# Attention and mixture of experts on one core: other token order inside a batch, gate weights stored in 16-byte pieces

## The chip, the cores and the metric

The kernel runs on one core of one Trainium2 chip. The metric is device time in microseconds (us); lower is better. A core has five engines with queues of their own: TensorE (PE; its weight loads are shown apart as PEld), VectorE (DVE), ScalarE (ACT), GpSimd (POOL) and SyncE (SP), which here issues most of the transfers. All transfers, whoever issues them, run on the same 16 DMA engines.

## The reference

Capped attention over 8 batches, 12 heads, 448 tokens and 64 columns a head; then one expert for each of the 3584 tokens, at most 80 tokens an expert.

```python
scores = cap * np.tanh((q @ k.T / 8) / cap)          # per batch and head
attn = softmax(scores)                               # over the keys
x = (attn @ v)  -> [3584 tokens, 768]
logits = x @ w_gate                                  # [3584, 8]
expert_idx = argmax(logits); gate_w = softmax(logits)[expert_idx]
for e in range(8):                                   # keep the 80 tokens with the largest gate_w
    h = relu(x[tok] @ w1[e]); out[tok] = gate_w[tok] * (h @ w2[e])
```

All other rows of the output are zero.

## The kernel before

**Attention stage (0 to some 391 us).** 48 steps, one for each batch b (8) and pair of heads (6). TensorE makes scores (`sc`, L1019) and products with the values (`av`, L1043); ScalarE does tanh and exp; GpSimd and VectorE add the row sums. SP loads `kt`, `qt` (three steps ahead) and `vr` (one ahead).

**Gate of a batch (8 times).** When the six 128x448 blocks `x` of a batch are there, TensorE multiplies them with the gate's weights (`lgp`), ScalarE copies the logits to `lgs` (96 partitions x 448 tokens), and TensorE turns them in four transposes (L1126): the tokens then stand on 112 partitions (`C`) and 4 columns (`NC`) of `lt`. In a transpose, the 96x112 piece of `lgs` is the stationary operand (the LDWEIGHTS), and the identity is the moving one. VectorE works out expert, sorting key (`kc`) and gate weight on those 112x4 numbers, and `gate_weights` stores the gate weights `g` in the list `gd` in memory (L322), one float for each of the 3584 tokens. For batches 0 to 6 SP issues this store, for batch 7 GpSimd does. Later each expert's rows of `x` (`xge`, `xgv`, from the copy `xs`) and of `gd` (`gt`, `gtv`) are gathered by token number. A constant table (`pa`, `pb`, from the number t4 = 4 (token + 1)) says which token stands at which partition and column.

**Expert stage (391 to 516 us).** Six experts' products in a fixed order, `hp` (x by w1) and `yt` (by w2), both issued at L758. Each takes its weights `w` from memory in 84 loads by SP (L746) of 512 or 384 KB, in a ring of buffers, each load waiting for the fifth before it. The last batch's gate, ranking and stores to `xs` (8 of them, from GpSimd's queue) go on beside this. The order of instructions on every engine is written out by the program, not by a scheduler that weighs costs.

The lines the steps touch are the view of `gd`, the transposes, and the store:

```python
gdv = gd.rearrange("(c p) a -> p (c a)", p=C)            # token = 112 c + p
nc.tensor.transpose(lt[:, c]..., lg[:, c * C:(c + 1) * C], cst("ident", 96)[:, :96])
queue.dma_start(gdst, g)                                 # gdst = gdv[:, 4 columns of batch b]
```

Of the kernel before, what the change touches and what calls it, by code (L numbers as in the profile page):

```python
# [17 lines left out]
B, H, S, D = 8, 12, 448, 64  # L18
NP = H // 2
NQ = H // 4  # L20
C = 112
# [3 lines left out]
NC = S // C  # L25
NB = S // 32
T = B * S
NCOL = T // C
DM = H * D
E = 8  # L30
# [52 lines left out]
def const_table():  # L83
    import numpy as np
    t = np.zeros((128, NCT), np.float32)

    def put(key, val):
        a, b = CT[key]
        t[:, a:b] = val
    p = np.arange(128)  # L90
    e = np.arange(E)
    put("pow", np.exp2(31.0 * e - 98.0)[None])
    put("rev", (E - e)[None])
    put("pre", (e < NPRE)[None])
    put("pen", (E * (e >= NPRE))[None])
    put("io", e[None])
    put("io32", np.arange(32)[None])
    put("io96", np.arange(SL)[None])
    put("lo3", np.array([[0, 32, 64]]))
    put("hi3", np.array([[32, 64, 96]]))  # L100
    put("slot", p[:, None])
    t4 = 4 * (p[:, None] + C * np.arange(NCOL)[None] + 1)
    put("pa", t4 // 256 * 256)
    put("pb", t4 % 256)
    put("blk", SL * np.arange(NBMAX)[None])
    put("gt", (e[None, :] > e[:, None]).reshape(1, -1))
    put("tri", np.where(np.arange(C)[None, :] >= p[:, None], -1.0, 0.0))
    put("rest", (T - C * (np.arange(NCOL) + 1))[None])
    put("ident", np.eye(128))
    return t  # L110
# [3 lines left out]
def attn_moe(ctx, tc, q2, k, v, cap, wg, w1, w2, capacity, ct, out):  # L114
    nc = tc.nc
# [4 lines left out]
    ohd = dram.tile([C, NCOL, E], F32, name="ohd")  # L120
    xs = dram.tile([T, 4, NP, 32], F32, name="xs")
    gd = dram.tile([T, 1], F32, name="gd")
    gdv = gd.rearrange("(c p) a -> p (c a)", p=C)

    fl_i = consts.tile([1, 2], I32, name="fl_i")
    big = consts.tile([1, 1], F32, name="big")
# [14 lines left out]
    def cst(key, n=128):  # L141
        a, b = CT[key]
        return ctt[:n, a:b]
# [6 lines left out]
    kc = consts.tile([C, NCOL], F32, name="kc")  # L150
    oh = consts.tile([C, NCOL, E], F32, name="oh")
    cms = consts.tile([C, OCOL], F32, name="cms")
    ohv = consts.tile([C, WCOL, E], F32, name="ohv")
    cmn = consts.tile([C, WCOL], F32, name="cmn")
# [3 lines left out]
    us = consts.tile([C, OCOL], F32, name="us")  # L158
# [677 lines left out]
    def attention_rowmax(sm, pl, b):  # L836
# [3 lines left out]
        for u in range(NQ):  # L840
            xp = [pl.tile([128, 512], F32, name=f"gxp{u}{f}", tag=f"gxp{f}") for f in range(2)]
            for h4 in range(4):
# [11 lines left out]
                for i in range(NC):  # L854
                    ps = pl.tile([C, 512], F32, name=f"gps{j}{h}{i}", tag="gps")
                    nc.tensor.matmul(ps[:, :S], qt[:, h, i * C:(i + 1) * C], kt[:, h, :], start=True, stop=True)
                    e = sm.tile([C, S], F32, name=f"ge{j}{h}{i}", tag="ge")
# [30 lines left out]
        lg = sm.tile([32, S], F32, name="glgs", tag="glgs")  # L888
        nc.vector.tensor_copy(lg, lgp[0:32, :S])
        lt = pl.tile([C, NC, 1, 32], F32, name="glt", tag="glg", bufs=2)  # L890
        for c in range(NC):
            nc.tensor.transpose(lt[:, c, 0], lg[:, c * C:(c + 1) * C], cst("ident", 32)[:, :32])
        kcb = sm.tile([C, NC], F32, name="gkc", tag="gkc")
        ohb = sm.tile([C, NC, E], F32, name="goh", tag="goh")
        for f in gate_math(sm, lt[:, :, :, 0:E], "g", kcb, ohb, gdv[:, bass.ds(b * NC, NC)]):
            f()
        nc.sync.dma_start(kcd[:, bass.ds(b * NC, NC)], kcb)
        nc.sync.dma_start(ohd[:, bass.ds(b * NC, NC)], ohb)
# [1 line left out]
    def general():  # L900
# [4 lines left out]
        with tc.If(bg > 0):  # L905
            with tc.tile_pool(name="gs", bufs=1) as sm:
                with tc.tile_pool(name="gp", bufs=1, space=PSUM) as pl:
                    with tc.For_i(0, B, 1) as b:
                        attention_rowmax(sm, pl, b)
                    nc.sync.dma_start(kc, kcd)  # L910
                    nc.sync.dma_start(oh, ohd)
# [48 lines left out]
    sm = at.enter_context(tc.tile_pool(name="sm", bufs=2))  # L960
# [8 lines left out]
    st = {"laid": set()}  # L969
# [4 lines left out]
    with ExitStack() as a2:  # L974
# [123 lines left out]
        def stored(q, b, i, js=slice(0, NB)):  # L1098
            q.dma_start(xs.rearrange("(b j a) i p c -> b i a j p c", b=B, j=NB)[b, i, :, js], st["xt", b][32 * i:32 * i + 32, js])
# [7 lines left out]
        def logits(b, js):  # L1107
            if js[0] == 0:
                st["lp", b] = ps1.tile([128, 512], F32, name=f"lgp{b}", tag="misc", bufs=2)
            for j in js:  # L1110
                g = j % 3
                nc.tensor.matmul(st["lp", b][32 * g:32 * g + 32, :S], wgt[:, j, :], st["x", b, j], start=(j < 3), stop=(j >= 3))

        def gate(b):
            def product():
                logits(b, range(NP))
                lp = st["lp", b]
                lg = sm.tile([96, S], F32, name=f"lgs{b}", tag="lgs", bufs=1)
                nc.scalar.copy(lg, lp[0:96, :S])
                st["lgs", b] = lg  # L1120

            def turn():
                lg = st["lgs", b]
                lt = ps1.tile([C, NC, 3, 32], F32, name=f"lt{b}", tag="misc", bufs=2)
                for c in range(NC):
                    nc.tensor.transpose(lt[:, c].rearrange("p g e -> p (g e)"), lg[:, c * C:(c + 1) * C], cst("ident", 96)[:, :96])  # L1126
                st["lt", b] = lt

            def math():
                cs = slice(b * NC, (b + 1) * NC)  # L1130
                lt = st["lt", b][:, :, :, 0:E]
                if b < OB:
                    st["math"] = gate_math(sm, lt, b, kc[:, cs], oh[:, cs], gdv[:, cs], us[:, cs], cms[:, cs])
                else:
                    ws = slice(b * NC - OCOL, (b + 1) * NC - OCOL)
                    st["math"] = gate_math(sm, lt, b, kc[:, cs], oh[:, cs], gdv[:, cs], None, cmn[:, ws], ohv[:, ws], nc.sync if b < B - 1 else nc.gpsimd)
            def end(pd):
                r = st["rank"] = consts.tile([C, RCOL], F32, name="rank")
                nc.vector.tensor_tensor(osd, osd, dfc2, op=ALU.add)
                nc.vector.tensor_reduce(r, acc2, axis=AX.X, op=ALU.add)  # L1140
                nc.vector.tensor_tensor(r, r, osd, op=ALU.subtract)
                n = pd.shape[-1]
                nc.vector.tensor_tensor(r[:, :n], r[:, :n], pd, op=ALU.subtract)
                st["chain"]()
            def later():
                st["math"][2]()
                if b < OB:
                    steps = list(ranks(krow, gp, ps1, "misc", b, acc, dfc, 0, 0, []))
                else:
                    steps = list(ranks(krow, gp, ps1, "misc", b, acc2, dfc2, CAND, OCOL, [e * SL for e in range(E)]))  # L1150
                if b == OB - 1:
                    kept = list(prune(krow, gp, ps1, "misc"))
                    n = next(i for i, x in enumerate(kept) if x[0] == 1750)
                    steps = [steps[0], kept[0], *steps[1:4], kept[1], *steps[4:7], kept[2], *steps[7:9], *kept[3:n], *steps[9:], *kept[n:]]
                if b > OB:
                    bg.insert(0, steps.pop(0))
                bg.extend(steps)
                now[2] = now[0]
                ready_at[2] = clock[1]

            def finish():
                st["math"][2]()
                steps = list(ranks(krow, gp, ps1, "misc", b, acc2, dfc2, CAND, OCOL, [e * SL for e in range(E)], end=end))
                f0, f1, f2, f6, f3, f4, f5, f8 = final_order(sm, lambda: ps1.tile([128, 512], F32, name="pcn", tag="misc", bufs=2))
                parts = [(50, lambda i=i, h=h: stored(nc.gpsimd, b, i, slice(NB // 2 * h, NB // 2 * h + NB // 2)), 1) for i in range(4) for h in range(2)]
                head = [(400, f0, 0), steps[0], (200, f1, 1), steps[1], (200, f2, 1), steps[2], (200, f6, 1), (200, f3, 0), steps[3],
                        steps[4], (300, f4, 1), *steps[5:8], (300, f5, 1), *steps[8:10], (300, f8, 1), *steps[10:]]
                n = 4
                for x in parts:
                    head.insert(n, x)  # L1170
                    n += 2
                bg.extend(head)
            st["wait"]()
            urgent.append((300, product, 0 if b < OB else 1))
            urgent.append((300, turn, 1 if b < OB else 2))
            if b < OB - 1:
                urgent.append((2500, lambda: (math(), st["math"][0](), st["math"][1](), later()), 1))
                return
            urgent.append((1900, lambda: (math(), st["math"][0]()), 1 if b < OB else "ordered"))
            urgent.append((1900, lambda: st["math"][1](), 0))  # L1180
            urgent.append((1000, finish if b == B - 1 else later, 0))
# [242 lines left out]
```

## Time and profile before

| | us |
|---|---|
| three runs: median (lowest to highest) | 524.43 (523.38 to 525.9) |
| the profiled execution | 523.92 |
| its span, first to last instruction | 522.1 |
| TensorE busy | 477.3 (91%) |
| VectorE / ScalarE / GpSimd busy | 344.2 / 328.6 / 257.4 |
| mean granted TensorE clock | 0.992 |

The profile is of one execution; 1.8 us of its time lie around the span. A busy TensorE is not one at its peak, since matmuls are pipelined. The profile's 40 slices of the span show TensorE busy in nine tenths or more of nearly each slice up to about 420 us, and 7 to 9 tenths behind that.

### The profile page before, as it was taken

To read this page: it belongs to the slowest core of one execution; us is meant where nothing else is said; L and a number is where in the kernel's file an instruction comes from. 1 tells how busy PE (TensorE), PEld (TensorE's weight loads), DVE (VectorE), ACT (ScalarE), POOL (GpSimd) and SP (SyncE) were. 2 spreads that over 40 slices of the span, in tenths; PEclk is the share of its full clock that TensorE was granted. 3 is DMA by queue.
4 is the path that set the end of the run, shared out by engine and by line. 5 is a ranking of instruction groups with operands and counts; after the bars stand their busy time and mean duration, and the time that the engine had idled before them with its cause. 6 is when DMAs were issued, how large, how long until landed. Compare 5 with 4: busy or idle time off the path is not lost. (4 is left out here: it accounts for less than half of the span.)

```text
span 522.1 us, 13512 instructions
## 1 busy us (share of the span) xinstructions
PE 477.3 (91%) x5476; PEld 218.7 (42%) x5476; DVE 344.2 (66%) x783; ACT 328.6 (63%) x326; POOL 257.4 (49%) x175
## 2 busy tenths in 40 slices
PE   6899999999899999999999998989999978887894
PEld 2223322332332323333323332233335778787894
DVE  1177789878988998899889866984669624512000
ACT  4998879788787978788777875857890101011111
POOL 0666657554664645576356443635964064043001
PEclk9999999999999999999999999989999998999999
DMA  6655359667765774578538769783659789999931
GB/s 165 184 167 148 92 105 222 173 187 87 199 212 131 105 231 108 94 143 251 131 87 163 166 157 257 120 216 106 196 109 315 239 220 407 381 383 398 361 127 45
DMA packets 74103, 99.03 MB, mean 190 GB/s; under 512 B 16976, under 2 KB 59248, under 8 KB 74032
## 3 DMA queue, kind: packets, MB, share of 16 engines
q1 hardware_dynamic: 72048, 93.45, 65.8%
q0 software_dynamic: 1984, 4.63, 2.8%
q8 instruction: 45, 0.74, 0.6%
q14 instruction: 26, 0.21, 0.2%
HBM read 74.54 MB, written 23.51 MB: 188 GB/s over the span
## 5 line engine op out<-in xcount | busy, mean ns | idle before, releaser
L1027 ACT ACTIVATE e<-sc,scl 128x896 f32<-128x896 f32 x168 | 162.4, 1005 | 55.0 <-PE sc L1019 53.0
L1043 PE MATMUL av<-e,vr 128*32 128x448 f32 x1536 | 174.3, 546 | 3.7 <-ACT e L1032 1.9
L1053 POOL TENSOR_TENSOR t<-t,e 128x896 f32<-128x896 f32 x48 | 109.4, 2279 | 92.6 <-ACT e L1032 85.6
L1032 ACT ACTIVATE e<-e,capt 128x1792 f32<-128x1792 f32 x96 | 153.6, 1601 | 0.0
L1019 PE MATMUL sc<-qt,kt 64*128 64x448 f32 x576 | 139.1, 585 | 12.5 <-ACT e L1027 7.5
L1051 POOL TENSOR_TENSOR t<-e 128x896 f32<-128x896 f32 x48 | 106.1, 2211 | 74.9 <-ACT e L1032 74.9
L1061 DVE SCALAR_TENSOR_TENSOR t<-t,e 64x448 f32<-64x448 f32 x68 | 93.0, 1378 | 29.7 <-ACT e L1032 28.5
L1043 PEld LDWEIGHTS av<-e,vr 128*32 128x32 f32 x1536 | 46.7, 109 | 100.8 <-issue 72.1
L1019 PEld LDWEIGHTS sc<-qt,kt 64*128 64x128 f32 x576 | 49.7, 191 | 89.8 <-issue 41.7
L408 DVE TENSOR_SCALAR_CACHE_REDUCE gb<-krow,kc 112x896 bf16<-112x896 f32 (+16 forms) x59 | 53.9, 930 | 8.0 <-ACT krow L388 4.4
L758 PE MATMUL yt<-thv,w 128*64 128x80 f32 x1152 | 44.5, 235 | 10.1 <-issue 10.1
L758 PE MATMUL hp<-xt,w 128*64 128x80 f32 x1152 | 44.7, 237 | 2.4 <-issue 2.4
L758 PEld LDWEIGHTS yt<-thv,w 128*64 128x64 f32 x1152 | 41.9, 137 | 12.0 <-issue 12.0
L758 PEld LDWEIGHTS hp<-xt,w 128*64 128x64 f32 x1152 | 42.5, 140 | 5.1 <-issue 4.8
L1073 DVE STREAM_TRANSPOSE st<-sp 128x448 f32<-128x448 f32 x24 | 15.5, 647 | 34.1 <-PE sp L1070 18.6
L802 POOL DMA_INDIRECT out_dram<-ysv,si x6 | 5.7, 956 | 56.0 <-ACT ysv L801 37.4
L1093 DVE STREAM_TRANSPOSE xb<-x 128x448 f32<-128x448 f32 x48 | 30.8, 644 | 1.6
L1068 PE MATMUL sp<-t,ones 128*32 128x448 f32 x192 | 28.2, 551 | 3.4 <-DVE t L1061 2.0
L774 ACT COPY ty0v<-yt 128x240 f32<-128x240 f32 x6 | 2.1, 358 | 46.1 <-PE yt L758 46.1
L1085 DVE TENSOR_TENSOR x<-av,r 128x448 f32<-128x448 f32 x48 | 29.5, 616 | 0.8
L1026 PE MATMUL sc<-qt,kt 64*64 64x448 f32 x192 | 23.6, 562 | 0.0
L774 DVE COPY ty1v<-yt 128x240 f32<-128x240 f32 x1 | 0.4, 408 | 33.8 <-ACT ty0v L774 33.8
(216 smaller groups left out, 302.9 us busy)
## 6 DMA issues: line engine op xcount, KB each, us to landing
w<-in_w_dram SPq DMA_DIRECT2D x36, 512.0 KB, 8.2
w<-in_w_dram SPq DMA_DIRECT2D x48, 384.0 KB, 6.0
kt<-in_k_dram SPq DMA_DIRECT2D x96, 112.0 KB, 3.6
qt<-in_q_dram SPq DMA_DIRECT2D x96, 112.0 KB, 2.8
xs<-xb SPq DMA_DIRECT2D x28, 336.0 KB, 5.9
vr<-in_v_dram SPq DMA_DIRECT2D x24, 256.0 KB, 3.6
out_dram<-zero SPq DMA_DIRECT2D x4, 1536.0 KB, 7.2
vr<-in_v_dram SPq DMA_DIRECT2D x24, 192.0 KB, 3.0
```

Source lines behind the costliest of these rows:

```text
L408: nc.vector.tensor_scalar(g, krow[:, x:y], kp, 0.0, op0=ALU.is_ge, op1=ALU.add, accum_out=a)
L758: nc.tensor.matmul(ps[j // per][64 * h:64 * h + 64, j % per * m:(j % per + 1) * m], w[:, 128 * j + 64 * h:128 * j + 64 * h + 64], x[:, kk, ...
L1019: nc.tensor.matmul(ps[:, h, :S], s["k"][w, x:x + CK], s["q"][w], start=True, stop=True)
L1027: nc.scalar.activation(s["e"][:, 2 * c:2 * c + 2], ps[:, :, :S], AF.Tanh, scale=scl)
L1032: nc.scalar.activation(x, x, AF.Exp, scale=capt)
L1043: nc.tensor.matmul(st["av", u, f][32 * g:32 * g + 32, :S], st[p]["v"][:, g % 2, c, 32 * f:32 * f + 32], late(p) if c == NK else st[p]["e"] ...
L1051: nc.gpsimd.tensor_tensor(t1, e[:, 0:2], e[:, 2:4], op=ALU.add)
L1053: nc.gpsimd.tensor_tensor(s["es"], s["es"], e[:, 4:6], op=ALU.add)
L1061: nc.vector.scalar_tensor_tensor(t1[w, h], t1[w, h], 0.0, late(p)[w], op0=ALU.add, op1=ALU.add)
L1068: nc.tensor.matmul(sp[32 * g:32 * g + 32, :S], ones[:, 0:32], s["es"][:, g % 2, :], start=True, stop=2 * u < RMB)
L1085: nc.vector.tensor_tensor(x, st["av", u, f][:, :S], st["r", u], op=ALU.mult)
L1093: nc.vector.transpose(st["xt", b][:, :, j, :], st["x", b, j].rearrange("p (a b) -> p a b", b=32))
```

## The change

A token's place changes inside its batch. Before, token t of a batch (0 to 447) stood on partition t mod 112, column t div 112; now it stands on partition t div 4, column t mod 4. Three things follow. The piece of `lgs` that a transpose loads is every fourth token, a stride of 4 floats (16 bytes), where it was 112 neighbours. The four gate weights of a partition are neighbours in `gd`, so the store of a batch is 112 pieces of 16 bytes, where it was 448 pieces of 4 bytes. The constant table, made on the host, gives the new token numbers. The comparisons of the ranking see the tokens in the new order.

```diff
-    t4 = 4 * (p[:, None] + C * np.arange(NCOL)[None] + 1)
+    col = np.arange(NCOL)[None]
+    t4 = 4 * (S * (col // NC) + NC * p[:, None] + col % NC + 1)
...
-    gdv = gd.rearrange("(c p) a -> p (c a)", p=C)
+    gdv = gd.rearrange("(b p c) a -> p b (c a)", b=B, p=C)
...
                 for c in range(NC):
-                    nc.tensor.transpose(lt[:, c].rearrange("p g e -> p (g e)"), lg[:, c * C:(c + 1) * C], cst("ident", 96)[:, :96])
+                    nc.tensor.transpose(lt[:, c].rearrange("p g e -> p (g e)"), lg.rearrange("p (t c) -> p c t", c=NC)[:, c], cst("ident", 96)[:, :96])
...
-                    st["math"] = gate_math(sm, lt, b, kc[:, cs], oh[:, cs], gdv[:, cs], us[:, cs], cms[:, cs])
+                    st["math"] = gate_math(sm, lt, b, kc[:, cs], oh[:, cs], gdv[:, b], us[:, cs], cms[:, cs])
...
-                    st["math"] = gate_math(sm, lt, b, kc[:, cs], oh[:, cs], gdv[:, cs], None, cmn[:, ws], ohv[:, ws], nc.sync if b < B - 1 else nc.gpsimd)
+                    st["math"] = gate_math(sm, lt, b, kc[:, cs], oh[:, cs], gdv[:, b], None, cmn[:, ws], ohv[:, ws], nc.sync if b < B - 1 else nc.gpsimd)
```

The same edit is made in the path for unusual inputs, which does not run here.

No instruction moves: on each engine the order is that of before, with one line added ahead of all of them, so that each line number is one higher. Only the shape of the store differs. On SP, at the store of batch 0, with the loads that stand behind it, before:

```order
L1099 DMA xs<-xb_363 32x14x192 x4
L322 DMA gd<-g_706 112x4x1
L990 DMA kt_712<-in_k_dram 64x448
L991 DMA qt_711<-in_q_dram 64x448
L990 DMA kt_712<-in_k_dram 64x448
L991 DMA qt_711<-in_q_dram 64x448
```

and now:

```order
L1100 DMA xs<-xb_363 32x14x192 x4
L323 DMA gd<-g_706 112x4
L991 DMA kt_712<-in_k_dram 64x448
L992 DMA qt_711<-in_q_dram 64x448
L991 DMA kt_712<-in_k_dram 64x448
L992 DMA qt_711<-in_q_dram 64x448
```

Nothing moved; the store has one dimension less. On GpSimd, at the store of batch 7, with the gathers of the fourth expert behind it, before:

```order
L322 DMA gd<-g_4274 112x4x1
L706 DMA xge_0_4303<-xs,gi_107 128x192
L706 DMA xge_1_4305<-xs,gi_107 128x192
L706 DMA xge_2_4307<-xs,gi_107 128x192
L605 DMA gt_110<-gd,sg_109 96x1
```

and now:

```order
L323 DMA gd<-g_4274 112x4
L707 DMA xge_0_4303<-xs,gi_107 128x192
L707 DMA xge_1_4305<-xs,gi_107 128x192
L707 DMA xge_2_4307<-xs,gi_107 128x192
L606 DMA gt_110<-gd,sg_109 96x1
```

Here too only the shape differs.

## Rows read from the trace of the kernel before

**Rows 1.** The page: bytes moved in 40 slices of the span, and all DMA packets

```profile
GB/s 165 184 167 148 92 105 222 173 187 87 199 212 131 105 231 108 94 143 251 131 87 163 166 157 257 120 216 106 196 109 315 239 220 407 381 383 398 361 127 45
DMA packets 74103, 99.03 MB, mean 190 GB/s; under 512 B 16976, under 2 KB 59248, under 8 KB 74032
```

**Rows 2.** Windows by stage: engines' busy time (instructions), PEclk, DMA share, GB/s

```profile
60.00:391.00 331.00, 315.30 (x2523) 105.86 (x2515) 271.16 (x589) 263.62 (x246) 186.85 (x89) 0.99 0.68 158
...
429.40:432.00 2.60, 0.19 (x3) 0.19 (x4) 1.11 (x3) 0.00 (x0) 0.00 (x0) 0.88 0.91 334
...
500.00:522.00 22.00, 14.61 (x372) 13.54 (x367) 1.02 (x2) 2.60 (x6) 1.83 (x2) 0.96 0.13 38
```

**Rows 3.** Windows: 8 us behind batch 7's store, and the expert stage after them

```profile
421.40:429.40 8.00, 6.69 (x161) 6.18 (x159) 2.69 (x6) 0.46 (x1) 5.12 (x13) 1.00 0.86 136
432.00:500.00 68.00, 58.47 (x1518) 55.74 (x1518) 17.05 (x69) 9.93 (x23) 18.80 (x34) 0.98 1.01 384
```

**Rows 4.** Windows of 2 us around batch 7's store

```profile
419.00:421.00 2.00, 2.00 (x55) 1.91 (x52) 0.00 (x0) 0.70 (x1) 1.70 (x2) 1.00 1.00 397
...
423.00:425.00 2.00, 1.31 (x39) 1.31 (x40) 1.73 (x3) 0.00 (x0) 0.88 (x4) 1.00 0.67 103
...
427.00:429.00 2.00, 1.84 (x54) 1.94 (x53) 0.38 (x1) 0.00 (x0) 1.30 (x5) 1.00 0.71 137
...
431.00:433.00 2.00, 1.19 (x18) 1.19 (x20) 1.95 (x2) 0.22 (x1) 0.00 (x0) 0.59 1.03 411
433.00:435.00 2.00, 2.00 (x38) 2.00 (x36) 2.00 (x4) 0.40 (x2) 0.67 (x3) 0.55 1.03 409
```

**Rows 5.** Windows of 2 us behind batch 0's store

```profile
75.00:77.00 2.00, 2.00 (x24) 0.75 (x24) 0.74 (x2) 2.00 (x4) 1.83 (x1) 1.00 0.42 14
...
79.00:81.00 2.00, 2.00 (x18) 0.61 (x18) 2.00 (x4) 1.67 (x2) 1.99 (x1) 1.00 0.61 34
...
83.00:85.00 2.00, 2.00 (x19) 0.85 (x17) 1.97 (x4) 2.00 (x2) 1.95 (x1) 1.00 0.87 244
```

**Rows 6.** The stores of the gate weights (line 322): ns min/median/max, first and last start

```profile
L322 SPq DMA_DIRECT2D gd<-g x7: 317/318/356, 74.9 to 378.9; - x7
L322 POOL DMA_DIRECT2D gd<-g x1: 784/784/784, 416.6 to 416.6; - x1
...
DMA to landing us min/median/max: 8.0/8.0/8.0
```

**Rows 7.** Timeline of TensorE behind that: start, us, instructions [idle before, releaser]

```profile
431.81 0.93 PE L758 MATMUL yt<-thv,w 128*64 128x80 f32 x9 [2.58 <-issue]
```

**Rows 8.** The chain that ended last, two pieces of 42: start, us, what

```profile
500.71 0.50 issue
501.20 7.00 PE yt L758 x195
```

**Rows 9.** Windows: later stores to xs beside the weights' loads

```profile
442.00:444.00 2.00, 1.02 (x30) 0.86 (x26) 0.23 (x1) 0.17 (x1) 1.78 (x5) 1.00 0.99 396
```

**Rows 10.** The transposes of the logits (line 1126): ns min/median/max

```profile
L1126 PEld LDWEIGHTS lt<-ctt,lgs x32: 130/132/137, 66.5 to 411.7; 96*112 96x112 f32 x32
L1126 PE MATMUL lt<-ctt,lgs x32: 244/246/296, 66.5 to 411.8; 96*112 96x96 f32 x32
```

**Rows 11.** Timeline at batch 0's transposes, TensorE and VectorE

```profile
65.55 4.25 DVE L1061 SCALAR_TENSOR_TENSOR t<-t,e 64x448 f32<-64x448 f32 x4 [1.72 <-ACT e L1032]
...
66.50 0.35 PEld L1126 LDWEIGHTS lt<-ctt,lgs 96*112 96x112 f32 x4 [0.65 <-ACT lgs L1119]
66.50 0.54 PE L1126 MATMUL lt<-ctt,lgs 96*112 96x96 f32 x4
...
69.72 0.24 DVE L293 TENSOR_REDUCE lg<-lt 112x32 f32<-112x96 f32 x1
```

**Rows 12.** VectorE's sums (line 264) that read every eighth float

```profile
L264 DVE TENSOR_REDUCE hs<-oh x1: 411/411/411, 274.1 to 274.1; 112x8 f32<-112x160 f32 x1
L264 DVE TENSOR_REDUCE hs<-ohv x1: 291/291/291, 417.6 to 417.6; 112x8 f32<-112x96 f32 x1
```

More of the change, by code (lines that the diff above doesn't have):

```diff
@@ L891, in attention_rowmax @@
         for c in range(NC):
-            nc.tensor.transpose(lt[:, c, 0], lg[:, c * C:(c + 1) * C], cst("ident", 32)[:, :32])
+            nc.tensor.transpose(lt[:, c, 0], lg.rearrange("p (t c) -> p c t", c=NC)[:, c], cst("ident", 32)[:, :32])
         kcb = sm.tile([C, NC], F32, name="gkc", tag="gkc")
         ohb = sm.tile([C, NC, E], F32, name="goh", tag="goh")
-        for f in gate_math(sm, lt[:, :, :, 0:E], "g", kcb, ohb, gdv[:, bass.ds(b * NC, NC)]):
+        for f in gate_math(sm, lt[:, :, :, 0:E], "g", kcb, ohb, gdv[:, bass.ds(b, 1)].rearrange("p b c -> p (b c)")):
             f()
```

## The prediction

> **What bounds the kernel now.** I read the page first, then windows by stage, then windows of 2 us around each store of the gate weights, then the timeline and the chain of waits. The bytes moved in 40 slices [rows 1] show two stages: up to slice 31 (some 400 us) around 150 GB/s, behind it about 400 until slice 38. In attention, TensorE is busy 315.3 of 331 us and the DMA engines 68% [rows 2]; TensorE sets the pace. In the expert stage from 432 to 500 us the DMA share is 1.01 at 384 GB/s, while TensorE is busy 58.5 of 68 us [rows 3]: there the loads of the weights set the pace and TensorE waits for them. The last such wait in the chain ends at 501.2 us, and TensorE runs from there almost without a gap [rows 8]; behind 500 us the DMA share is 0.13 [rows 2]. So what brings the whole stream of weights forward brings the end forward, until TensorE's own work (9.5 us less than the stretch from 432 to 500) binds.
>
> In that stream there is a hole. GpSimd issues the store of batch 7 at 416.6 us [rows 6]. Until 421 us the DMA moves 397 GB/s; at 423 to 429 it moves 103 to 137; from 431 on 411 and 409 [rows 4]. Over 8 us the mean is 136 GB/s [rows 3]. [...]
>
> Is the hole the store's work? The seven stores that SP issues show the same without any gather beside them. Behind batch 0's store at 74.9 us, with loads of `kt`, `qt` and `vr` right behind it in the queue, the DMA moves 14 to 34 GB/s at a share of 0.42 to 0.61, and 244 again from 83 us [rows 5]: again 8 us, and the store itself takes 8.0 us to land [rows 6]. 448 pieces in 8.0 us are 18 ns a piece, however they are spread over the engines. Bytes are not it: 448 floats are 1,792 bytes.
>
> **The change, part by part.**
>
> *The seven stores on SP.* 448 pieces become 112, each four times as long. If the price goes by pieces, the hole shrinks from 8.0 to 2.0 us. In attention I cost this at nothing: the loads held up are those of three steps ahead, and TensorE is busy 2.00 of 2 us in each of these windows [rows 5]. Without that cover it would be up to 7 times 6 us.
>
> *The store on GpSimd.* The same 6.0 us of the hole vanish where the DMA is the bound. What that gives is the shortfall against the rate right behind the hole, 410 GB/s [rows 4]: 8.0 us x (1 - 136/410) = 5.35 us of lost transfer time [rows 3, 4]. Three quarters of it: 4.0 us. Bounds: 0, if a 16-byte piece holds the memory four times as long as a 4-byte one; 5.35, if it holds nothing. I take 4.0, since the seven stores of equal length on another queue say that something is paid per piece, and nothing in the rows shows a price per byte at this size. Passed on in full, because all weights behind it come 4.0 us earlier, and TensorE has 9.5 us of waits between 432 and 500 us to give up [rows 3]. GpSimd's 784 ns for the issue [rows 6] may fall a little; the gathers behind it wait for the DMA anyway, so nothing.
>
> [...]
>
> *The 32 strided weight loads.* The four transposes of a batch load every fourth float. A load now takes 132 ns and a matmul 246 [rows 10]; four of each take 0.35 and 0.54 us [rows 11]. So loads follow each other every (0.35 - 0.13)/3 = 73 ns and matmuls every (0.54 - 0.25)/3 = 98 ns: a load may take 25 ns longer for nothing. No TensorE read with a stride stands in the trace. From below: nothing. From above, the nearest strided read is VectorE's, of every eighth float: (411 - 291) ns / 64 elements = 1.88 ns an element [rows 12]. At that, 112 columns take 210 ns, 112 more than the 98 of now; 28 loads ahead of the expert stage give 3.1 us. Between them, a load twice as long (146 ns apart) costs 48 ns x 28 = 1.3 us. I take 0.4, nearer to nothing: most of the load's 132 ns is not its columns' spacing of 73, so that a slower read shows only in part. VectorE does not care: the transposes end at 67.0 us, and it reads `lt` at 69.72, being busy with its own sums until 69.8 [rows 11]. Batch 7's four loads delay the start of the hole, not the stream.
>
> The one price of a strided read in the rows, 1.88 ns an element, is VectorE's [rows 12]. [...]
>
> *The table and the ranking* cost nothing: the table is made on the host, and comparisons take the same time for any order of their data.
>
> **Sum.** On the profiled execution (span 522.1 us, 1.8 around it, 523.92 in all): 523.9 - 4.0 + 0.4 = 520.3. The median of the three runs is 0.5 above that execution, so I forecast **520.8 us** as a median. Its own range is 519 to 522.
>
> **Rivals.**
>
> 1. *The hole stays, or the end does not follow it.* For: the gathers of `xge` and the stores to `xs` begin in the same microseconds as the hole, and 16 bytes are still a small write. Against: later stores to `xs` run at 396 GB/s with the weights [rows 9], and the holes of attention have no gathers [rows 5]. Time: 523.9 + 0.4 + 0.5 = 524.8. [...]
> 2. *The strided loads take back most of it*, at VectorE's price: 523.9 - 4.0 + 3.1 + 0.5 = 523.5. For: [rows 12]. Against: another engine, another stride.
> [...]
>
> **Chances.** A measurement of this kernel can tell about 0.5% (2.6 us) from no change: below 521.8 is faster, above 527.1 slower. The forecast has 0.58 (the 18 ns a piece stand on eight stores; the passing on is less sure), rival 1 0.24, rival 2 0.10, rival 3 0.08. Faster 0.58, same 0.34, slower 0.08. The range for 8 in 10 goes from 518.6 (the whole 5.35 us and free loads: 519.1, less half a us of scatter) to 525.0, which takes in rivals 1 and 2 and leaves out rival 3.
>
> **What would show it.** DMA packets fall by 7 x 336 = 2352, to 71751, if pieces on SP's queue are counted one by one, and those under 512 B to 14624 [rows 1]. The 2-us windows behind each store show over 150 GB/s after 2 to 3 us in place of 8, and the landing falls from 8.0 to 2 to 4 us. Between 421 and 429 us the DMA moves over 300 GB/s; TensorE's wait of 2.58 us goes or shrinks; the last wait of the chain ends near 497 us. [...] Wrong if the hole stays at its 8 us, or if the stream comes early and some other wait (a buffer, the ranking on VectorE, GpSimd's gathers) holds the end.

## The result, and the profile after

| | before | changed |
|---|---|---|
| median (22 runs of each) | 525.32 us | 521.29 us |
| lowest to highest | 522.38 to 531.38 us | 514.75 to 525.29 us |
| profiled execution | 523.92 us | 520.92 us |
| its span | 522.1 us | 519.1 us |

The ratio is 0.990 (0.9875 to 0.9924), taken over the executions of the faster of two states, without four slow ones of the changed kernel. The medians of all runs differ by 4.0 us, 0.8%. In the changed file each line number of the program's body is one higher than before (line 322 is 323, and so on).

The page first: the bytes moved in 40 slices and the packets, which answer to [rows 1].

```profile
GB/s 165 183 178 147 92 114 267 116 189 164 121 211 135 163 165 112 102 230 167 113 105 214 103 154 271 181 161 79 225 110 258 255 358 404 353 388 400 366 65 45
DMA packets 71751, 99.03 MB, mean 191 GB/s; under 512 B 14624, under 2 KB 56896, under 8 KB 71680
```

The packets fell by 2352, exactly the 7 x 336 of the seven stores; GpSimd's pieces are not among those counted. The 33rd slice (415 to 428 us), where the hole of batch 7's store lay, reads 358; before's 33rd has 220. The windows over the same stretches as [rows 3, 4] show it closely (us; busy time of PE, PEld, DVE, ACT, POOL with instructions; PEclk, DMA share, GB/s):

```profile
421.40:429.40 8.00, 6.69 (x175) 6.25 (x171) 6.38 (x11) 0.30 (x2) 5.21 (x16) 1.00 1.02 357
432.00:500.00 68.00, 58.41 (x1518) 55.74 (x1518) 12.51 (x55) 9.24 (x21) 18.14 (x31) 0.97 0.94 355
...
423.00:425.00 2.00, 2.00 (x58) 2.00 (x60) 1.72 (x5) 0.00 (x0) 0.87 (x3) 1.00 0.97 299
...
427.00:429.00 2.00, 1.00 (x30) 0.84 (x28) 2.00 (x4) 0.00 (x0) 1.65 (x7) 1.00 1.02 399
...
431.00:433.00 2.00, 2.00 (x43) 1.72 (x39) 0.27 (x4) 1.04 (x2) 0.00 (x0) 1.00 1.04 415
433.00:435.00 2.00, 1.35 (x39) 1.25 (x37) 0.00 (x0) 0.00 (x0) 1.75 (x3) 1.00 1.02 410
```

Read the last column: in the 8 us where before moved 136 GB/s the changed kernel moves 357, and the dip that is left is one window of 299. The last two rows are granted the full clock, where before had 0.59 and 0.55. The fall of the DMA share from 432 to 500 us (1.01 before, 0.94 now) says that the stream of weights now ends before the stretch does: the last of the 84 loads is issued at 491.97 us, where before it was at 496.85. The stores themselves, to be compared with [rows 6], and the windows after batch 0's store, to be compared with [rows 5]:

```profile
L323 SPq DMA_DIRECT2D gd<-g x7: 327/331/368, 74.2 to 378.4; - x7
L323 POOL DMA_DIRECT2D gd<-g x1: 587/587/587, 416.2 to 416.2; - x1
...
DMA to landing us min/median/max: 1.4/2.4/6.4
```

```profile
75.00:77.00 2.00, 2.00 (x24) 0.79 (x20) 1.36 (x5) 2.00 (x4) 1.58 (x1) 1.00 0.43 39
77.00:79.00 2.00, 2.00 (x16) 0.69 (x8) 1.93 (x6) 1.61 (x2) 0.68 (x1) 1.00 0.60 174
79.00:81.00 2.00, 2.00 (x20) 0.59 (x20) 2.00 (x3) 2.00 (x3) 1.42 (x1) 1.00 0.93 271
81.00:83.00 2.00, 2.00 (x16) 0.65 (x18) 1.94 (x8) 2.00 (x2) 0.64 (x1) 1.00 1.09 388
```

Batch 0's store landed in 8.0 us before, the only one whose landing that trace has; here it takes 2.4 us. (Of the other two with a landing here, batch 5's took 1.4 us, and batch 7's, which GpSimd issues, 6.4.) From 79 to 81 us the DMA moves 271 GB/s, where before had 34. TensorE is busy 2.00 of 2 us here as it was before, so these stretches give nothing back. The transposes, which answer to [rows 10, 11], became dearer:

```profile
L1127 PEld LDWEIGHTS lt<-ctt,lgs x32: 180/204/205, 65.8 to 411.3; 96*112 96x112 f32 x32
L1127 PE MATMUL lt<-ctt,lgs x32: 268/270/345, 65.8 to 411.4; 96*112 96x96 f32 x32
```

```profile
65.81 0.66 PE L1127 MATMUL lt<-ctt,lgs 96*112 96x96 f32 x4
```

A load takes 204 ns, 72 more; four matmuls take 0.66 us, 0.12 more. TensorE's standstill of [rows 7] shrank from 2.58 to 1.00 us:

```profile
428.59 0.56 PE L759 MATMUL yt<-thv,w 128*64 128x80 f32 x9 [1.00 <-issue]
```

Last the chain of waits that ended last, to be compared with [rows 8]. Before:

```profile
459.83 0.45 PE pcp L679 x12
...
460.67 3.47 PE hp L758 x96
...
513.73 0.02 issue
```

And now:

```profile
455.51 0.45 PE pcp L680 x12
...
456.35 5.11 PE hp L759 x96
...
492.56 0.83 issue
493.38 3.05 PE hp L759 x82
...
505.59 4.74 PE yt L759 x132
```

The matmuls `pcp` start 4.3 us earlier than before. The same 96 matmuls `hp` behind them took 3.47 us before and take 5.11 now: TensorE's clock is granted at 0.51 and 0.64 in this stretch, as these windows show (0.50 from 457.1 to 460.3 us alone), and at 1.00 at 431 us.

```profile
457.00:459.00 2.00, 2.00 (x36) 2.00 (x34) 0.86 (x6) 0.07 (x1) 0.89 (x1) 0.51 1.01 400
459.00:461.00 2.00, 2.00 (x42) 2.00 (x40) 0.00 (x0) 0.00 (x0) 1.39 (x3) 0.64 1.03 399
```

The last wait of the chain ends at 493.38 us (501.20 before), and from there TensorE works without a gap until 510.33 us. It ended its matmuls on weights at 513.73 before: 3.4 us earlier in this execution.

**What TensorE waits for in this stage.** The prediction took these waits for waits for weights. The traces of both kernels speak against it. Every load of weights whose landing they show was in SBUF 12 us or more before TensorE's first matmul on it. The standstill of 2.58 us falls in the middle of the 24 matmuls on one buffer, a load that was issued at 404.26 us. The waits come at matmuls that are a multiple of 128 apart (give or take two), eight of them at the same matmul in both kernels, and nearly all end shortly after a packet of 16 KB on a DMA queue of its own, the one that the page lists as `q8 instruction` (45 packets, 0.74 MB, in both kernels). The first wait behind the store, and the six of before that are over 1 us:

| TensorE matmuls done | before: packet ends | TensorE goes on, after a wait of | changed: packet ends | TensorE goes on, after a wait of |
|---|---|---|---|---|
| 3465 | 422.29 | 423.70, 0.69 | 421.50 | 422.94, 0.31 |
| 3593 | 430.53 | 431.81, 2.58 | 427.29 | 428.59, 1.00 |
| 3848 | 442.69 | 444.08, 1.06 | 438.97 | 440.30, 1.04 |
| 3976 | 448.54 | 450.00, 1.33 | 444.98 | 446.22, 1.33 |
| 4487 | 471.70 | 473.18, 2.10 | 467.79 | 469.13, 1.17 |
| 4615 | 478.22 | 479.75, 1.19 | 474.67 | 475.97, 1.46 |
| 4997 | 494.84 | 496.06, 1.10 | 492.10 | 493.38, 0.83 |

In the fourteen traces of this document TensorE stands still for more than 0.25 us, and waits for nothing that the profile shows, 127 times between 418 and 510 us. Of these waits 123 end 1.2 to 1.6 us after such a packet; the other four lie in holes behind stores of 4-byte pieces. So TensorE waits here for its own instructions, which the profile counts among the packets of the same DMA engines. After the weights' last loads the packets go on and such waits are gone (the last one ends at 501.20 us before, at 493.38 now). All this is read from the times; no run changed the loading of the instructions alone. At the hole, the packet before the standstill started 7.5 us after the one ahead of it (428.80 after 421.32) and took 1.73 us; in the changed kernel it was 5.8 us (426.29 after 420.53) and 1.00 us.

### The profile page after: what moved, and what is told of

It reads as the page before. It is cut to its first block, busy times and chain, and to the rows that moved or that the text cites. A ratio compares the mean times of both kernels' runs of the same rounds, so it can differ in the third digit from the quotient of the medians.

```text
span 519.1 us, 13512 instructions
## 1 busy us (share of the span) xinstructions
PE 477.7 (92%) x5476; PEld 219.3 (42%) x5476; DVE 344.0 (66%) x783; ACT 328.6 (63%) x326; POOL 257.0 (49%) x175
## 5 line engine op out<-in xcount | busy, mean ns | idle before, releaser
L1020 PE MATMUL sc<-qt,kt 64*128 64x448 f32 x576 | 137.7, 579 | 11.6 <-ACT e L1028 6.1
L759 PE MATMUL yt<-thv,w 128*64 128x80 f32 x1152 | 43.3, 234 | 6.3 <-issue 6.3
L769 ACT ACTIVATE thv<-hp 128x640 f32<-128x640 f32 x6 | 4.2, 704 | 30.7 <-PE hp L759 26.4
```

What stands on the lines that cost most here:

```text
L759: nc.tensor.matmul(ps[j // per][64 * h:64 * h + 64, j % per * m:(j % per + 1) * m], w[:, 128 * j + 64 * h:128 * j + 64 * h + 64], x[:, kk, ...
L1020: nc.tensor.matmul(ps[:, h, :S], s["k"][w, x:x + CK], s["q"][w], start=True, stop=True)
```

## Experiments

Edits are on the changed kernel where nothing else is said. Each ratio is to the kernel before, run on the same chip, with its interval; where there is no interval, there was one execution.

**1. Are the short pieces the cause, and in which store?** Each of the first three puts `g` in every second float, so that the same values in the same order leave as 448 pieces of 4 bytes again: in all stores, in the seven of SP alone, and in batch 7's alone.

```diff
-        g = sm.tile([C, NC], F32, name=f"g{b}", tag="g")
+        g = sm.tile([C, NC, 2], F32, name=f"g{b}", tag="g")[:, :, 0]
```

(In the second and the third run the new tile stands only where `queue` is `nc.sync`, or `nc.gpsimd`.) All stores:

> The changed kernel with its order of tokens and its strided loads, but with g written into every second float of a tile, so that no two gate weights are neighbours at the source and all eight stores go out in 448 pieces of 4 bytes to the same places. If the price is per piece: holes of 8 us again, packets back to 74103, and the gain is gone but for the strided loads' own cost, ratio to the kernel before 1.000 to 1.003. If it is the new order of the places in memory that helps, or something else of the change: ratio 0.990, holes stay at 2 to 3 us.

The seven of SP:

> As the run with 4-byte pieces everywhere, but only for the seven stores that SP issues in attention; batch 7's store keeps its 16-byte pieces. If the gain is that of batch 7's store in the expert stage: ratio 0.989 to 0.992, as the changed kernel, though the holes behind the seven stores are 8 us long. If the holes of attention cost time: ratio 0.995 or more, up to 1.000.

Batch 7's:

> The other half: only batch 7's store, which GpSimd issues, goes out in 4-byte pieces; the seven of attention have 16-byte pieces. If the gain is that of batch 7's store: ratio 0.999 to 1.003, a hole of 8 us at 421 to 429 us, the wait of TensorE of some 2.5 us back. If it is attention's: ratio near 0.990.

Measured: all stores 528.5 us, ratio 1.0084 (1.0047 to 1.012); SP's seven 523.31 us, 0.997 (0.9926 to 1.0013); batch 7's alone 530.48 us, 1.0147 (1.0092 to 1.0202). The windows of 2 us behind batch 7's store, in the third and then in the second:

```profile
423.00:425.00 2.00, 1.50 (x39) 1.34 (x41) 2.00 (x4) 0.00 (x0) 0.81 (x2) 1.00 0.96 42
425.00:427.00 2.00, 1.66 (x47) 1.50 (x44) 0.11 (x3) 0.00 (x0) 1.71 (x5) 1.00 0.73 33
427.00:429.00 2.00, 0.23 (x1) 0.13 (x1) 0.00 (x0) 0.00 (x0) 1.05 (x5) 1.00 0.93 131
429.00:431.00 2.00, 1.38 (x18) 1.26 (x19) 0.00 (x0) 0.00 (x0) 0.49 (x1) 0.59 0.91 145
431.00:433.00 2.00, 2.00 (x38) 2.00 (x36) 0.76 (x2) 0.00 (x0) 0.15 (x1) 0.56 0.69 144
```

```profile
423.00:425.00 2.00, 1.79 (x34) 1.51 (x33) 0.59 (x2) 0.53 (x1) 1.26 (x3) 1.00 1.01 376
```

Cutting up batch 7's store alone brings the hole back, longer than before (some 10 us against 8), with the low clock behind it, and makes the kernel slower than before. Cutting up the seven on SP brings back their holes in attention (32, 48 and 39 GB/s at 77 to 83 us) and none at batch 7. So the gain lies in one store, that of batch 7. Whether the attention's holes cost anything needed a second set of runs with the same edit:

> The run with 4-byte pieces in the seven stores of SP alone, once more; it came out at 0.997 (0.9926 to 1.0013), between the two theories. If attention's holes cost nothing: 0.988 to 0.993, equal to the changed kernel. If they do cost about 3 us: 0.995 to 1.000 again.

It took 522.78 us, 0.9934 (0.9892 to 0.9975), again with a hole after batch 0's store (36 to 43 GB/s from 77 to 83 us) and none at batch 7:

```profile
423.00:425.00 2.00, 1.11 (x27) 0.95 (x29) 2.00 (x4) 0.00 (x0) 0.81 (x2) 1.00 1.01 336
```

The times alone don't settle it. The first interval (0.9926 to 1.0013) lies just above that of the changed kernel (0.9875 to 0.9924), the second overlaps it, and on the second's chip a kernel without any hole (the old order with spread pieces, in part 3) came out at the same 0.993. The traces settle it for the first five of the seven stores. From the transposes of one batch to those of the next, up to batch 5, it takes:

| kernel | from batch to batch, us |
|---|---|
| before (holes) | 47.42, 47.18, 48.97, 48.26, 54.64 |
| changed (no holes) | 47.42, 47.19, 48.97, 48.26, 54.64 |
| 4 bytes in every store (holes) | 47.40, 47.19, 48.95, 48.25, 54.62 |

So the holes cost nothing there. (The runs with a second tile for `g` have up to 0.2 us more a step, with holes in attention or without: 47.50, 47.27, 49.10, 48.33, 54.70 us for the run that cut up batch 7's store alone.) The next two steps can't be read from single executions: they differ by up to 1.9 us between the traces, and for the first of them two executions of the changed kernel have 53.2 and 51.7 us.

**2. The strided loads.** ScalarE's copy of the logits out of PSUM writes them sorted by column, so that the transposes read neighbours again.

```diff
-                lg = sm.tile([96, S], F32, name=f"lgs{b}", tag="lgs", bufs=1)
-                nc.scalar.copy(lg, lp[0:96, :S])
+                lg = sm.tile([96, NC, C], F32, name=f"lgs{b}", tag="lgs", bufs=1)
+                nc.scalar.copy(lg.rearrange("p c t -> p t c"), lp[0:96, :S].rearrange("p (t c) -> p t c", c=NC))
...
-   nc.tensor.transpose(..., lg.rearrange("p (t c) -> p c t", c=NC)[:, c], ...)
+   nc.tensor.transpose(..., lg[:, c], ...)
```

> The changed kernel, but ScalarE's copy of the logits writes them already sorted into four rows of 112, so that the transposes load neighbours. LDWEIGHTS there fall from 204 to 132 ns, the four matmuls from 0.66 to 0.54 us. If these 0.12 us a batch are on the path in attention: 0.8 us less than the changed kernel, ratio 0.988 to 0.990. If ScalarE pays more for the scattered write than TensorE for the strided read (527 ns before, to 900 ns at a doubled price): ratio 0.990 to 0.994.

It took 521.46 us, 0.9901 (0.986 to 0.9943): the same as the changed kernel. The rows show what was traded:

```profile
L1127 PEld LDWEIGHTS lt<-ctt,lgs x32: 131/132/137, 66.4 to 411.4; 96*112 96x112 f32 x32
...
L1120 ACT COPY lgs<-lgp x8: 912/922/955, 65.4 to 408.3; 96x448 f32<-96x448 f32 x8
```

Loads are back at 132 ns, and the copy takes 922 ns where it took 527. From batch to batch, as in the table above, the steps up to batch 5 are 47.40, 47.19, 48.95, 48.25 and 54.46 us here. Those of before (no stride) and of the changed kernel (stride) agree within 0.01 us: there the stride costs nothing that can be seen. Over all of attention, from the first transposes to those of batch 7, single executions have 344.8 us here, 345.2 with the stride and 345.0 before, but the second execution of the changed kernel has 343.6, so no cost can be taken from these totals.

A finer question is how the load depends on the stride. Here the copy leaves pairs of floats together, so that a load takes every second float, and finds two of them in each 16 bytes:

```diff
-                lg = sm.tile([96, S], ...)
-                nc.scalar.copy(lg, lp[0:96, :S])
+                lg = sm.tile([96, 2, C, 2], ...)
+                nc.scalar.copy(lg.rearrange("p h t j -> p t h j"), lp[0:96, :S].rearrange("p (t h j) -> p t h j", h=2, j=2))
...
+   nc.tensor.transpose(..., lg[:, c // 2, :, c % 2], ...)
```

> The changed kernel with ScalarE's copy writing the logits in pairs, so that a transpose loads every second float (8 bytes) in place of every fourth (16 bytes). With every fourth a load took 204 ns, with neighbours 132. If what counts is how many floats of 16 bytes one load uses: two of four, 132 ns or little more. If any stride is dear: about 204 ns.

```profile
L1127 PEld LDWEIGHTS lt<-ctt,lgs x32: 181/202/207, 66.2 to 410.1; 96*112 96x112 f32 x32
```

One execution took 519.55 us. A load of every second float takes 202 ns, as long as one of every fourth (204 ns), though it finds two of its floats in each 16 bytes and that one a single float. If the number of floats used of 16 bytes were what counts, the load would have been back near 132 ns. The measurement decides: these loads of the stationary matrix pay for either stride, and the same (70 and 72 ns on top of 132).

**3. What is the price of a store?** First the changed kernel once more on another chip, as the standard for the runs beside it.

> The changed kernel once more, on the same chip as the next three, so that they are compared with it and not with an earlier chip. Ratio to the kernel before 0.988 to 0.993, hole behind batch 7's store of 2 us, last wait of the chain 4 us earlier than before.

520.83 us, 0.9892 (0.9847 to 0.9937). Then batch 7's store in 224 pieces of 8 bytes:

```diff
+        if queue is nc.gpsimd:
+            g = sm.tile([C, 2, 3], F32, name=f"g{b}", tag="g7")[:, :, 0:2]
+            w2 = w2.rearrange("p (a c) e -> p a c e", a=2)
...
-        queue.dma_start(gdst, g)
+        queue.dma_start(gdst.rearrange("p (a c) -> p a c", a=2) if queue is nc.gpsimd else gdst, g)
```

> The changed kernel, but batch 7's store goes out in 224 pieces of 8 bytes (g stands in SBUF in pairs with a gap). If the price is per piece: a hole of half of that of 448 neighbouring pieces (about 5 us of the 10 to 11 seen there), and a time halfway between the changed kernel and the one with 4-byte pieces for batch 7, ratio 0.998 to 1.004. If only pieces of a single float are dear: no hole over 2 us, ratio 0.990.

It took 524.21 us, 0.9947 (0.9913 to 0.9981). That lies between the changed kernel and the one with 448 pieces, though below the 0.998 to 1.004 that were expected, and its hole of some 5 us lies between theirs too:

```profile
423.00:425.00 2.00, 1.38 (x35) 1.21 (x37) 1.98 (x4) 0.00 (x0) 0.81 (x2) 1.00 0.91 144
425.00:427.00 2.00, 2.00 (x66) 2.00 (x62) 0.51 (x4) 0.00 (x0) 1.70 (x4) 1.00 0.89 210
427.00:429.00 2.00, 1.68 (x50) 1.51 (x44) 0.38 (x1) 0.00 (x0) 1.64 (x6) 1.00 0.95 333
```

So far a price for each piece fits. But in all these runs the pieces also lie closer the more there are. The next keeps the 448 pieces of 4 bytes in every store and puts each weight 64 bytes from the next in HBM; the list is cleared once, and the indices of the gathers are multiplied by 16.

```diff
-    gd = dram.tile([T, 1], F32, name="gd")
-    gdv = gd.rearrange("(b p c) a -> p b (c a)", b=B, p=C)
+    gd = dram.tile([T * 16, 1], F32, name="gd")
+    gdv = gd.rearrange("(b p c k) a -> p b c (k a)", b=B, p=C, k=16)[:, :, :, 0]
...
+        nc.vector.tensor_scalar(sg, sg, 16.0, None, op0=ALU.mult)
```

> The changed kernel with the list gd spread out: 64 bytes from one gate weight to the next, so all eight stores have 448 pieces of 4 bytes again, but no two within 64 bytes. Gather indices are times 16, and the longer list is set to zero once in the first steps. If the price is per piece, wherever it lands: holes of 8 us or more, ratio 1.000 or more. If it is paid for pieces that land close together: holes of 2 to 3 us or less, ratio 0.989 to 0.994.

It took 521.3 us, 0.9881 (0.9844 to 0.9919). The windows behind batch 7's store, and the stores' rows:

```profile
423.00:425.00 2.00, 0.61 (x18) 0.61 (x20) 1.75 (x4) 0.00 (x0) 0.87 (x4) 1.00 1.03 365
425.00:427.00 2.00, 2.00 (x65) 2.00 (x61) 1.03 (x4) 0.00 (x0) 1.83 (x5) 1.00 1.06 374
```

```profile
L323 POOL DMA_DIRECT2D gd<-g x1: 762/762/762, 416.5 to 416.5; - x1
...
DMA to landing us min/median/max: 2.9/3.1/3.4
```

448 pieces of 4 bytes, and no hole like those before (318 and 311 GB/s at 427 to 431 us are the lowest): neither the number of pieces nor their size is enough to make it. Nor do the pieces hold the DMA engines themselves for long. After batch 0's store in the kernel before, from 75.70 to 77.00 us, the trace has

```profile
DMA packets 479, 0.03 MB, mean 22 GB/s; under 512 B 464, under 2 KB 479, under 8 KB 479
```

and nearly all of its 448 pieces start within 0.5 us; then the DMA moves 34 to 47 GB/s until 83 us. In the run with pieces 64 bytes apart they start within 0.5 us as well, and the loads after them move at once (203 GB/s from 77 to 79 us, 268 from 79 to 81). What is left is how close the pieces land. If so, the kernel before needs no new order of the tokens, only the distance. This edit is on the kernel before, with its order and its loads of neighbours:

```diff
-    gd = dram.tile([T, 1], F32, name="gd")
-    gdv = gd.rearrange("(c p) a -> p (c a)", p=C)
+    gd = dram.tile([T * 16, 1], F32, name="gd")
+    gdv = gd.rearrange("(c p k) a -> p c (k a)", p=C, k=16)[:, :, 0]
```

> The kernel before with its own order of tokens and its unstrided loads, and only the list gd spread out to 64 bytes a gate weight (gather indices times 16, the list set to zero once). If pieces are dear only where several land within 64 bytes: no holes with 448 pieces, ratio 0.985 to 0.992, as good as the changed kernel or half a us better, since the loads of the transposes stay at 132 ns. If the new order of tokens is needed for the gain: ratio 0.996 to 1.002.

```profile
423.00:425.00 2.00, 1.83 (x35) 1.51 (x33) 0.55 (x2) 0.53 (x1) 1.22 (x3) 1.00 1.00 364
425.00:427.00 2.00, 1.32 (x38) 1.33 (x40) 1.86 (x5) 0.00 (x0) 0.88 (x3) 1.00 1.04 365
```

It took 521.53 us, 0.993 (0.9895 to 0.9964), without a hole: a little above the first range, below the second. The distance alone gives the gain in the old order too. It is not measurably better than the changed kernel: the intervals overlap. Last, how close is close? The same edit as at 64 bytes with 16 and with 32 (`k=4` and `k=8`):

> The changed kernel with 448 pieces of 4 bytes, 16 bytes from one to the next, so that four of them share 64 bytes, as four of the 16-byte pieces do. If pieces that share 64 bytes wait for each other in a row, and different stretches run side by side: a hole of 2 to 3 us, as with 16-byte pieces. If every piece that shares pays in one common row: 448 of them, a hole of 8 us.

> The same with 32 bytes from one piece to the next, two to 64 bytes. If stretches of 64 bytes are what counts, by rows side by side: a hole of about 1 to 2 us or none that can be told. If stretches of 32 bytes count: none, and 16 bytes apart gives only 1 to 2 us. If sharing pays in one common row: 4 us or more.

There is one execution of each, 522.41 us at 16 bytes and 522.19 at 32, too few to compare times. Behind batch 7's store, at 16 and then at 32:

```profile
423.00:425.00 2.00, 1.83 (x52) 1.83 (x54) 1.71 (x3) 0.00 (x0) 0.87 (x4) 1.00 0.99 243
```

```profile
423.00:425.00 2.00, 1.49 (x42) 1.49 (x44) 1.87 (x5) 0.00 (x0) 0.87 (x3) 1.00 1.01 326
```

Side by side, GB/s in the window from 79 to 81 us (behind batch 0's store, on SP) and from 423 to 425 us (behind batch 7's, on GpSimd), each from the profile of that kernel:

| store | starts of pieces apart | pieces in 64 bytes | 79:81 | 423:425 |
|---|---|---|---|---|
| before: 448 of 4 bytes | 4 | 16 | 34 | 103 |
| 4 bytes in every store, new order | 4 | 16 | 39 | 56 |
| 4 bytes in batch 7's alone, new order | 4 | 16 | - | 42 |
| batch 7's: 224 of 8 bytes | 8 | 8 | - | 144 |
| changed: 112 of 16 bytes | 16 | 4 | 271 | 299 |
| 448 of 4 bytes | 16 | 4 | 69 | 243 |
| 448 of 4 bytes | 32 | 2 | 214 | 326 |
| 448 of 4 bytes | 64 | 1 | 268 | 365 |

In both columns the rate is low at 4 bytes and high from 32 on, whether there are 112 or 448 pieces. In between the windows scatter, since they lie at fixed times and the stores do not: with 112 pieces of 16 bytes, six executions have 148 to 271 in the first column and six have 242 to 376 in the second. So for batch 7's store the rises from 4 to 8 and to 16 bytes can be told, and those beyond cannot. In attention, 448 pieces 16 bytes apart do worse (69) than 112 in all six executions, so there their number counts as well. The list gets longer with the distance, so "few pieces in the same 64 bytes" and "pieces spread over a longer stretch" can't be told apart by these runs.

## Why the prediction was right

**The number.** 520.8 us were forecast and 521.29 measured; the medians differ by 4.0 us, where 4.0 less 0.4 were taken. In part this is luck, since two steps of the way to it were wrong (below).

**The place.** Batch 7's store was the one that counted, and its hole was the cost. This is shown by the runs that cut up one group of stores at a time (1.0147 with batch 7's, 0.997 and 0.9934 with the other seven) and by the old order with its pieces spread out (0.993).

**What failed: the path to the end.** "TensorE waits for them" and "Passed on in full, because all weights behind it come 4.0 us earlier" are not what the traces show. The weights did come early: the loads after the hole are issued 4.1 to 6.5 us earlier than before, the last one 4.9. But they lie in SBUF for 12 us or more before they are used, and TensorE's 9.5 us of waits are, by their times and as far as they are over 0.25 us, waits for its own instructions, but for one of 1.2 us for GpSimd's `rh` before `pcp`. The hole held the instructions up. TensorE was 0.8 us ahead of before's times at 422.94 us, 3.2 us after the standstill (428.59 against 431.81) and 4.3 us at `pcp`; then 4.0 at 469.13, 2.7 at 493.38 and 3.4 at its last matmul on weights. So of the 3.4 us some 2.5 arise at the standstill itself, and the rest is what the later waits, which differ by up to 0.9 us between the two kernels, add and take. "Until TensorE's own work binds" did not come into it.

**What failed: the reason for the size,** "If the price goes by pieces", with "18 ns a piece, however they are spread over the engines". 448 pieces set 64 bytes apart leave no hole, so there is no fixed price of a piece, and the pieces themselves take half a microsecond to go out. In the changed kernel fewer pieces also meant pieces farther apart, and so the two reasons gave the same number. Rival 1 (the hole stays) fell with the windows; its reason, the gathers and stores to `xs` in the same microseconds, fell with the spread pieces, where they run as before.

**The clock** has no term in the sum; its low stretch moved from 431 us (0.59 and 0.55) to 457 (0.51 and 0.64), where 96 matmuls took 1.6 us longer. The wait behind them became shorter (1.17 us in place of 2.10), and TensorE is 4.0 us ahead again where that wait ends. The lead that is lost after it, down to 2.95 us at 482.17, falls in waits for instructions (1.46 and 1.55 us, where before had 1.19 and 0.73), with the clock at 1.00.

**The seven stores** were costed at nothing, and for the first five the steps from batch to batch agree with and without holes within 0.02 us. Their holes did shrink.

**The strided loads**: 0.4 us were taken; the steps from batch to batch show 0.01 us or less for each of the first five. That one load takes 204 ns was not foreseen; it comes close to the 210 ns behind rival 2's 3.1 us. Of the 72 ns more, 25 were said to be hidden behind the matmuls: 47 ns for each of the three loads that follow the first make 0.14 us, and four matmuls took 0.12 us longer. But seven such groups, 0.8 us, do not appear in the steps. Rival 2's 3.1 us are out, and so is the slower time, which had a chance of 0.08.

**The ranking** was said to take the same time for any order of its data. The two orders that ran do: VectorE's comparisons of 112x896 numbers take 1132 ns (mean of 25) in both kernels, and those of 112x1664 1932 and 1931 ns (mean of 4). Other orders were not run.

**GpSimd's issue** fell from 784 to 587 ns with no consequence that the trace shows.

**Open:** what makes close pieces dear, and up to what distance (the rates are low at 4 bytes and high from 32 on, by the table); why attention's store at 16 bytes apart does worse than batch 7's; why close pieces in the new order, where neighbours come from one partition, are dearer than before's (528.5 and 530.48 us against 527.46); and what sets the time at which TensorE's next instructions are fetched.

## What to carry to other kernels

Look at the GB/s in windows of 2 us behind every small store: here 1,792 bytes held up the other transfers for 8 us, and it cost time only where TensorE was waiting for a transfer. Look which transfer that is: before a wait is put down to the weights, compare when their load landed with when they are used, and see whether the waits come at the same instruction count in every kernel: here eight did in both, and 123 of 127 ended 1.2 to 1.6 us after a packet of instructions. Before the work is reordered to merge the pieces, try to put them farther apart (64 bytes each was enough here): it needs one rearrangement and a factor on the indices. When two explanations of a hole give the same number for a change, find the run in which they differ.

## What the runs showed of the hardware that was not expected

- 448 pieces of 4 bytes side by side leave the DMA at 32 to 48 GB/s from 77 to 83 us in attention, and at 33 to 145 beside the loads of the weights; the same 448, 64 bytes apart, leave it at 364 to 374 there (423 to 427 us). The pieces themselves start within 0.5 us.
- TensorE's instructions come, as the times of its waits say, in packets of 16 KB (45 in either kernel), one for some 128 matmuls with their weight loads, beside the weights. While the weights move at 384 GB/s it waits 0.3 to 2.6 us for many of them, and goes on 1.2 to 1.6 us after the packet's end.
- LDWEIGHTS of 112 columns in fp32: 132 ns for neighbours, 202 for every second float, 204 for every fourth.
- ScalarE's copy of 448 floats a partition: 527 ns as they stand, 560 with pairs sorted, 922 with single floats sorted.
- GpSimd's issue of a store: 784 ns for 448 pieces in the old order and 762 to 765 in the new, 721 for 224, 587 to 590 for 112.
